# Two buffers of P in the last two pairs, the third for raw weights, and later turns for weight preparation

## The chip, the cores and the metric

One core of one Trainium2 chip runs the whole program in one launch. The metric is device microseconds of one execution. Matrix products run on TensorE (PE), elementwise work on VectorE (DVE), ScalarE (ACT) and GpSimd (POOL); every DMA is issued by SyncE (SP), one queue in program order. A time counts as changed if it moves by more than 0.5%, about 3.8 us here.

## The reference, cut to what matters

```python
# attention, 2 batches x 8 heads, 768 tokens, head size 64
q_bits = (q @ proj) > 0            # 6 bits: a bucket for each query and each key
mask   = q_bucket[:, None] == k_bucket[None, :]
P      = softmax(where(mask, q @ k.T / 8, -1e9))
x      = P @ v                     # as 1536 tokens x 512
# two feed-forward layers, 512 -> 2048 -> 512
y   = leaky(x @ moe_w_in, 0.01)  @ moe_w_out
out = prelu(y @ moe2_w_in, alpha) @ moe2_w_out
```

The program is handed the four weight matrices in float64, the rest in float32; it reads the two 32-bit words of a weight with integer operations.

## The kernel before

**Attention.** Heads go in 8 pairs (NP = 8), a pair being two heads of one batch; a pair has 12 score tiles, numbered `g = 12 * i + m`, so there are N = 96 of them. A tile (`score`) is 128 queries by 768 keys of one head: scores on PE, a capped minimum on DVE (L717), the exponential on ACT (L720). Then its P is turned over, keys onto partitions: either by three PE transposes and an ACT copy out of PSUM, twice (L736, L741), or by a split into a float16 high and low part (L754, L758, L760) and a DMA transpose (L766). A pair has two halves of 384 queries (f = 0, 1). The turned-over P of a half fills one tile of the ring `pt`, three buffers of 4608 words a partition, taken in turn (L703). `pv` multiplies it by v (L807, L816) and DVE writes x (L823); after that the buffer is free. Below, pv(6,1) is the product for pair 6, half 1.

**Feed-forward.** `ffn` walks 16 units (layer l, quarter fq of the 2048 hidden columns, batch b). A unit multiplies x by the quarter's w_in (`product`, L1163 to L1166, output named h, or y where it lies in the second bank of a y tile), applies the leaky step, and the next unit's steps take turns with the unit's own products with w_out (`y_group`). Where fq is 0 a unit uses the four blocks of x as they are (B11, B21, B12, B22); where it isn't, seven products that also need sums of blocks (T1 to T4, `x_sum`, L1150). Each block is split into two float16 parts (`x_keep`, `halves`: ACT L1087, DVE L1089).

**Group preparation.** The weights come in 16 groups, one for each layer, quarter and matrix: group 0 is the first quarter of the first w_in, group 1 that of the first w_out. `convert(n, claim, step, early)` loads four raw 512 KB tiles (L987), makes float32 of each (ACT L993; DVE L995, L999, L1002, L1005), finds one power of two for the group (`power`: DVE L933 to L944, a diagonal on ACT or POOL, a PE product L950, DVE L954 to L959), and splits the weights with it (L1087, L1089). Groups 0 and 1 convert one raw tile at a time, the others two.

**Memory is lent on.** When the attention has no more use for a buffer, the feed-forward takes it: raw tiles of groups 0 and 1 take three slots of `wraw`, then four of pt buffer 2, then the first of `wraw` again. So three tiles of group 0 lie in `wraw`, its fourth and three of group 1 in pt buffer 2. Split w_out lies in pt buffer 1, and some of the activations in pt buffer 0. Sixteen halves through three buffers: the last user of buffer 2 is pv(7,0), of buffer 1 pv(6,1), of buffer 0 pv(7,1).

**Who sets the order.** Every step is an operation added to a plan with a claim, possible engines with a modelled duration, what it reads and writes, and a turn (the claim unless given). `link` walks operations by claim: this fixes who waits for whom on a buffer. `first` builds a schedule from the modelled durations; among ready operations of one engine that could start within a short span, the lowest turn goes first. `late` and `early` then move each operation as late as its users allow and as early as its engine allows, by turns; of all schedules the one with the earliest modelled end is kept (`order`), and each engine's instructions are issued in its order. The chip follows that order whatever the real durations are.

Claims of the feed-forward start at N + 10 = 106. Before the change group 0 has claim 104 (its first three tiles 36), group 1 claim 105; conversion takes those claims as turns:

```python
convert(0, at - 2, 0.2, N - 60)
convert(1, at - 1, 0.2)
```

Of the kernel before, what the change touches and what calls it, by code (L numbers as in the profile page):

```python
# [43 lines left out]
LEAN_V, LEAN_X, LEAN_W = 0.0,0.0,0.0  # L44

X_LEAD, CONV = 30, (2, 5, 19, 6)
START, XAT = 10.0, (1, 9)
# [258 lines left out]
def lsh_attention_ffn_kernel(  # L306
# [13 lines left out]
    nc = tc.nc  # L320
# [51 lines left out]
    hl_r = ring("hl", 2)  # L372
    pt_r = ring("pt", 3)

    def fixed(shape, dtype, name, p=const):
# [318 lines left out]
    def score(g):  # L694
# [6 lines left out]
        if (i, f) not in sums:  # L701
            sums[i, f] = sum_r.new([128, TH, 2], F32, "sum")
            pts[i, f] = pt_r.new([128, 4 * T, HALF], F16, "pt")  # L703
        sm, pt = sums[i, f], pts[i, f]
# [172 lines left out]
    class Bank:  # L877
# [8 lines left out]
        def ap(self, w=HALF):  # L886
# [14 lines left out]
    thin_slots = Slots(list(zip(small[0::2], small[1::2])))  # L901
    w_outs = views(pt_at[1], 2 * T * HALF, DM)[:2 * FQ]
    o_slots = Slots(list(zip(w_outs[0::2], w_outs[1::2])))
# [3 lines left out]
    gv = [v for b in s_at[1:] for v in views(b, S, HALF // 2)]  # L907
    gv += views(pt_at[0], 2 * T * HALF, HALF // 2)[:16]
    g_slots = Slots(list(zip(gv[0::2], gv[1::2])))
    h_slots = Slots([v for b in (s_at[0], *v_at) for v in views(b, S, HALF)]  # L910
                    + [View(pt_at[0], 8 * HALF + n * HALF, HALF) for n in range(4)])
    m_slots = Slots(views(on(m_r, 0, DM), DM, DM))
    m_pairs = Slots(views(on(hl_r, 1, 2 * S), 2 * DM, 2 * DM))

    def bank(ring):
        return Bank(ring.new([128, 1, HALF], F32, "h"), 0)
# [7 lines left out]
    def power(claim, cols_, most, most_use, scale_, scale_use, extra=None, reads=(), writes=(), wide=False, to=2.0**13):  # L924
# [3 lines left out]
        mx = mx_r.new([128, 1], F32, "mx")  # L928
        ps = b_banks.take() if claim >= N + 2 else bank(t_ps)
        buf, n = cols_  # L930
# [31 lines left out]

        plan.add(claim, vec(0.95 if extra else 0.8, scales), [ps.use(), *reads], [most_use, scale_use, *writes])

    def convert(n, claim, step, early=None):

# [4 lines left out]
        for k in range(FQ // per):  # L971
            j = k * per
            first = claim + j * step if early is None or j == FQ - 1 else early
            now = claim + j * step
            r, m = (r_slots.take(), m_slots.take()) if per == 1 else (r_pairs.take(), m_pairs.take())
            each = [View(r.buf, r.c0 + a * 2 * DM, 2 * DM) for a in range(per)]
            for a, one in enumerate(each):
# [16 lines left out]
                out=m.ap(F32), in_=high().bitcast(F32), func=AF.Abs)), [r.use()], [m.use()], turn=now)  # L994
            plan.add(first, vec(0.24 + w * 0.00052, lambda m=m, k=k: nc.vector.tensor_scalar(  # L995
                out=m.ap(F32), in0=m.ap(F32), scalar1=F64_MAX, scalar2=F64_MIN, op0=ALU.min,
                op1=ALU.max, accum_out=mw.t[:, k:k + 1]), True),
                [m.use()], [m.use(), col(mw, k)], turn=now)
            plan.add(first, vec(0.18 + w * 0.00052, lambda m=m: nc.vector.tensor_scalar(  # L999
                out=m.ap(I32), in0=m.ap(I32), scalar1=3, scalar2=0x3FFFFFFF,  # L1000
                op0=ALU.logical_shift_left, op1=ALU.bitwise_and), True), [m.use()], [m.use()], turn=now)
            plan.add(first, vec(0.19 + w * 0.00104, lambda m=m, low=low: nc.vector.scalar_tensor_tensor(  # L1002
                out=low(), in0=low(), scalar=29, in1=m.ap(I32), op0=ALU.logical_shift_right,
                op1=ALU.bitwise_or), True), [m.use(), r.use()], [r.use()], turn=now)
            plan.add(first, vec(0.19 + w * 0.00104, lambda low=low, high=high: nc.vector.scalar_tensor_tensor(  # L1005
                out=low(), in0=high(), scalar=-0x40000000, in1=low(), op0=ALU.bitwise_and,
# [39 lines left out]
        for p in range(0, FQ, 2):  # L1046
# [16 lines left out]
            for out_, x, y, op, to, frm in (  # L1063
                (s1, a21, a22, ALU.add, r1, r2), (s3, a11, a21, ALU.subtract, r2, r1),
                (s2, s1, a11, ALU.subtract, r1, r1), (s4, a12, s2, ALU.subtract, r2, r1),
            ):
                def add(out_=out_, x=x, y=y, op=op, eng=None):
                    eng.tensor_tensor(out=out_(), in0=x(), in1=y(), op=op)
                plan.add(claim, [
                    vec(0.37, lambda add=add: add(eng=nc.vector), True),  # L1070
                    gps(0.7, lambda add=add: add(eng=nc.gpsimd))], [r1.use(), r2.use()], [to.use()])
            halves(claim, wide, lambda r1=r1: r1.ap(F32).rearrange("p (d two) -> p two d", two=2),
# [72 lines left out]
    def x_sum(b, nm, claim, turn):  # L1145
# [3 lines left out]
        op = ALU.add if nm == "T2" else ALU.subtract  # L1149
        plan.add(claim, [vec(0.95, lambda: nc.vector.tensor_tensor(out=o(), in0=x(), in1=y(), op=op), True),  # L1150
                         gps(1.9, lambda: nc.gpsimd.tensor_tensor(out=o(), in0=x(), in1=y(), op=op))],
# [31 lines left out]
    def leaky(u, f, n, claim, src, src_use, own=None):  # L1183
# [7 lines left out]
        else:  # L1191
            plan.add(claim, act(0.58, lambda: nc.scalar.activation(
                out=g.ap(F32), in_=src(), func=AF.Copy, scale=low_by.t[:, f:f + 1])),
                [src_use, low_by], [g.use()])
            plan.add(claim, vec(0.56, lambda: nc.vector.scalar_tensor_tensor(  # L1195
                out=g.ap(F32), in0=src(), scalar=high_by.t[:, f:f + 1], in1=g.ap(F32),
# [130 lines left out]
    def ffn():  # L1327
# [5 lines left out]
        for u in [(l, fq, b) for l in range(2) for fq in range(NFQ) for b in range(B)]:  # L1333
            l, fq, b = u
            m = l * NFQ + fq
            if b == 0 and m == 0:
                convert(0, at - 2, 0.2, N - 60)
                convert(1, at - 1, 0.2)
            if b == 0 and m + 1 < 2 * NFQ:
# [80 lines left out]
```

## Time and profile before

| | us |
|---|---|
| three runs: median (lowest to highest) | 761.66 (761.4 to 764.04) |
| the profiled execution | 758.8 |
| its span, first to last instruction | 757.0 |
| PE busy (idle) | 705.5 (51.5) |
| DVE, ACT, POOL busy | 624.1, 487.7, 312.9 |

Attention fills the span up to about 252 us, the feed-forward the rest. PE is busy for 93% of the span and nowhere fully idle for long, so the time can only change by what stands between its instructions, or by its clock.

### The profile page before, as it was taken

What the parts mean: (1) busy time and instruction counts of PE and PEld (TensorE: products, weight loads), DVE (VectorE), ACT (ScalarE), POOL (GpSimd) and SP (SyncE); (2) the same over time, 40 slices, a digit from 0 to 9 for tenths busy, and PEclk for the clock granted to TensorE, in tenths of its full rate; (3) what the DMA queues carried; (4) which work ended last, traced back from release to release, by engine and by line L of the source; (5) the groups of instructions that cost most, each with busy time, mean ns of one, the idle gap of its engine ahead of it and who ended that gap; (6) DMA issues with size and microseconds to landing.
All of it is one profiled execution on the core that took longest, in us unless ns stands there. A gap on an engine that the chain in (4) does not pass through costs nothing.

```text
span 757.0 us, 12700 instructions
## 1 busy us (share of the span) xinstructions
PE 705.5 (93%) x4727; PEld 448.2 (59%) x4727; DVE 624.1 (82%) x1105; ACT 487.7 (64%) x903; POOL 312.9 (41%) x316
## 2 busy tenths in 40 slices
PE   7789978988987799999999999999999999999997
PEld 5577767877876556655565556555454555555553
DVE  6889898788899987879888886999997989986442
ACT  5887878897889676666656545565675764654340
POOL 2776757866564052213332532324043324333220
PEclk9989999999999899999999999999999999999999
DMA  7597997988757430331322313120311212100012
GB/s 208 126 197 166 194 197 168 221 173 177 157 129 145 171 103 9 111 113 41 106 77 74 95 56 111 34 78 1 112 52 60 84 59 82 55 1 2 15 55 98
DMA packets 131214, 77.89 MB, mean 103 GB/s; under 512 B 100864, under 2 KB 123392, under 8 KB 131152
## 3 DMA queue, kind: packets, MB, share of 16 engines
q1 hardware_dynamic: 131152, 77.08, 39.3%
q8 instruction: 37, 0.61, 0.3%
q14 instruction: 25, 0.20, 0.1%
HBM read 43.00 MB, written 3.15 MB: 61 GB/s over the span
## 4 chain that ended last, share of the span: by engine, by line
PE 66%; DVE 25%; ACT 4%; issue 3%; POOL 1%; DMA 0%; SPq 0%; DVEq 0%; POOLq 0%
PE y L1164 10%; PE y L1166 10%; PE y L1165 10%; PE sc L710 7%; PE h L1164 6%; PE h L1166 6%; PE h L1165 6%; DVE ff L1089 4%; PE o L807 3%; DVE s L717 3%; PE pp L736 2%; PE o L816 2%; DVE ff L995 2%; DVE ff L1002 2%; DVE hl L760 2%
## 5 line engine op out<-in xcount | busy, mean ns | idle before, releaser
L416 POOL TENSOR_TENSOR ff<-ff 128x384 f16<-128x384 f32 x128 | 138.4, 1095 | 282.2 <-ACT ff L1198 241.9
L1164 PE MATMUL y<-ff 128*128 128x384 f16 (+1 forms) x496 | 171.9, 347 | 9.4 <-DVE ff L1209 2.8
L1166 PE MATMUL y<-ff 128*128 128x384 f16 (+1 forms) x496 | 171.8, 346 | 0.0
L1165 PE MATMUL y<-ff 128*128 128x384 f16 (+1 forms) x496 | 171.8, 346 | 0.0
L1164 PE MATMUL h<-ff 128*128 128x384 f16 x416 | 136.3, 328 | 2.9 <-ACT ff L1087 2.8
L1165 PEld LDWEIGHTS <-ff 128*128 128x128 f16 x912 | 89.4, 98 | 81.1 <-issue 14.9
L1166 PE MATMUL h<-ff 128*128 128x384 f16 x416 | 136.2, 327 | 0.7 <-DVE ff L1089 0.7
L1165 PE MATMUL h<-ff 128*128 128x384 f16 x416 | 136.1, 327 | 0.0
L1164 PEld LDWEIGHTS <-ff 128*128 128x128 f16 x912 | 89.3, 98 | 71.3 <-ACT ff L1087 2.9
L1166 PEld LDWEIGHTS <-ff 128*128 128x128 f16 x912 | 89.3, 98 | 70.6 <-DVE ff L1089 1.1
L717 DVE TENSOR_SCALAR_CACHE_REDUCE s<-sc 128x768 f32<-128x768 f32 x96 | 89.6, 951 | 19.1 <-PE sc L710 13.1
L720 ACT ACTIVATE s<-s,mn 128x768 f32<-128x768 f32 x96 | 89.6, 935 | 13.2 <-DVE s L717 12.5
L1298 DVE SCALAR_TENSOR_TENSOR x<-y,back,x 128x384 f32<-128x384 f32 (+1 forms) x84 | 56.3, 670 | 37.9 <-PE y L1166 35.1
L1198 ACT CAST ff<-ff 128x384 f16<-128x384 f32 x128 | 64.6, 510 | 23.2 <-DVE ff L1195 21.2
L1205 ACT COPY ff<-h 128x384 f32<-128x384 f32 x72 | 34.1, 477 | 56.1 <-PE h L1166 55.0
L710 PE MATMUL sc<-ka,qa 128*128 128x384 f32 x192 | 59.8, 394 | 8.8 <-DVE s L717 8.6
L416 POOL TENSOR_TENSOR hl<-s,hl 128x768 f16<-128x768 f32 x31 | 53.1, 1712 | 30.0 <-ACT hl L754 29.9
L710 PE MATMUL sc<-kb,qb 76*128 76x384 f32 x192 | 51.7, 350 | 0.2 <-ACT kb L613 0.2
L1089 DVE SCALAR_TENSOR_TENSOR ff<-ff,by 128x512 f16<-128x512 f32 (+2 forms) x54 | 48.1, 919 | 3.3 <-ACT ff L1087 3.1
L1087 ACT ACTIVATE ff<-ff,by 128x512 f16<-128x512 f32 (+2 forms) x54 | 43.7, 863 | 10.0 <-DVE by L959 8.2
L807 PE MATMUL o<-pt,vb 128*64 128x256 f16 (+1 forms) x576 | 48.2, 276 | 0.0
L1002 DVE SCALAR_TENSOR_TENSOR ff<-ff 128x1024 int32<-128x1024 int32 (+1 forms) x36 | 45.9, 1275 | 0.8
(142 smaller groups left out, 1207.2 us busy)
## 6 DMA issues: line engine op xcount, KB each, us to landing
ff<-in_moe_w_in_dram SPq DMA_DIRECT2D x32, 512.0 KB
ff<-in_moe_w_out_dram SPq DMA_DIRECT2D x32, 512.0 KB
v<-in_v_dram SPq DMA_DIRECT2D x8, 384.0 KB
out_dram<-x SPq DMA_DIRECT2D x12, 256.0 KB
k<-in_k_dram SPq DMA_DIRECT2D x7, 384.0 KB
q<-in_q_dram SPq DMA_DIRECT2D x7, 384.0 KB
kb<-ka SPq DMA_DIRECT2D x14, 192.0 KB
qb<-qa SPq DMA_DIRECT2D x14, 192.0 KB
```

The lines of the kernel that those rows point to most:

```text
L416: nc.gpsimd.tensor_tensor(out=o, in0=a, in1=b, op=ALU.subtract)
L710: nc.tensor.matmul(sc.t[:, h, 0:HALF], lhsT=o[a].t[0:rows, row:row + 128], rhs=o[b].t[0:rows, h * HALF:h * HALF + HALF], start=(n == 0), s ...
L717: plan.add(g, vec(1.03, lambda: nc.vector.tensor_scalar(out=s.t.rearrange("p (a b) -> p a b", a=2), in0=sc.t[:, :, 0:HALF], scalar1=FILL, ...
L720: plan.add(g, act(1.12, lambda: nc.scalar.activation(out=s.t, in_=s.t, func=AF.Exp, scale=-1.0, bias=mn.t[:, 0:1], accum_out=sm.t[:, t, j: ...
L807: nc.tensor.matmul(ps.t[64 * j:64 * j + 64, 0:split], lhsT=vb.t[:, piece, j, c, :], rhs=narrow(pt, i, f)[:, 2 * T * j + o + c], start=(c + ...
L1002: plan.add(first, vec(0.19 + w * 0.00104, lambda m=m, low=low: nc.vector.scalar_tensor_tensor(out=low(), in0=low(), scalar=29, in1=m.ap(I3 ...
L1089: plan.add(claim, vec(0.2 + w * 0.00108, lambda: nc.vector.scalar_tensor_tensor(out=part(lo), in0=src(), scalar=c(), in1=part(hi), op0=ALU ...
L1164: nc.tensor.matmul(ps, lhsT=lh[0], rhs=rh[0], start=first, stop=False, skip_group_check=skip)
L1165: nc.tensor.matmul(ps, lhsT=lh[0], rhs=rh[1], start=False, stop=False, skip_group_check=skip)
L1166: nc.tensor.matmul(ps, lhsT=lh[1], rhs=rh[0], start=False, stop=last, skip_group_check=skip)
L1198: plan.add(claim, act(0.51, lambda: nc.scalar.copy(out=gh.ap(), in_=g.ap(F32))), [g.use()], [gh.use()])
L1298: plan.add(claim, vec(0.69 if l else 0.56, lambda: nc.vector.scalar_tensor_tensor(out=a(), in0=ps.ap(w), scalar=c(), in1=a(), op0=ALU.mult ...
```

## The change

It has five parts.

1. From pair 6 on, the turned-over P takes buffers 0 and 1 in turn; buffer 2 is used last by pv(5,1). The split w_out moves from buffer 1 to 0, the activations from 0 to 1. Buffer 0's last user is now pv(7,0), buffer 1's pv(7,1).
2. `EARLY`: group 0 has claim 88 and its fourth raw tile claim 78; group 1 keeps claim 105 but its raw tiles have claims 80, 80, 80, 90. The turn of the conversions of both is 104 (of their loads 98); what follows in `convert`, the power of two and the split, has the claim as its turn: 88.6 to 88.8 for group 0.
3. `LAG`: in groups 2 to 15 every operation but the loads has its turn 6 later.
4. Modelled durations of nine kinds of operation are changed.
5. The PE product of `power` no longer takes the two second banks of the y tiles in turn with the units' own use: group scales always take the first, the others the second. Group 0's takes a bank of the ring ps_t, as its claim lies before N + 2.

```diff
+LAG = 6
+EARLY = (88, 0.2, (36, 36, 36, 78)), (105, 0.2, (80, 80, 80, 90))
...
+    pt_late = part(pt_r, 0, 1)
...
-            pts[i, f] = pt_r.new([128, 4 * T, HALF], F16, "pt")
+            pts[i, f] = (pt_r if i < NP - 2 else pt_late).new([128, 4 * T, HALF], F16, "pt")
...
-    w_outs = views(pt_at[1], 2 * T * HALF, DM)[:2 * FQ]
+    w_outs = views(pt_at[0], 2 * T * HALF, DM)[:2 * FQ]
...
-    gv += views(pt_at[0], 2 * T * HALF, HALF // 2)[:16]
+    gv += views(pt_at[1], 2 * T * HALF, HALF // 2)[:16]
...
-                    + [View(pt_at[0], 8 * HALF + n * HALF, HALF) for n in range(4)])
+                    + [View(pt_at[1], 8 * HALF + n * HALF, HALF) for n in range(4)])
...
-        ps = b_banks.take() if claim >= N + 2 else bank(t_ps)
+        ps = b_banks.got[0 if wide else 1] if claim >= N + 2 else bank(t_ps)
...
-    def convert(n, claim, step, early=None):
+    def convert(n, *args):
+        first = len(plan.ops)
+        convert_now(n, *args)
+        for op in plan.ops[first:]:
+            if n > 1 and op.ways[0][0] != "SP":
+                op.turn += LAG
+
+    def convert_now(n, claim, step, early=None):
...
-            first = claim + j * step if early is None or j == FQ - 1 else early
-            now = claim + j * step
+            first = claim + j * step if early is None else early[j]
+            now = N + 8 if per == 1 else claim + j * step
...
-                convert(0, at - 2, 0.2, N - 60)
-                convert(1, at - 1, 0.2)
+                convert(0, *EARLY[0])
+                convert(1, *EARLY[1])
```

The changed durations, in us, w being the columns (512 or 1024): L995 from 0.24 + 0.00052 w to 0.2 + 0.00105 w, L999 from 0.18 + 0.00052 w to 0.13 + 0.00071 w, L1002 and L1005 from 0.19 + 0.00104 w to 0.13 + 0.00123 w and 0.13 + 0.0012 w; the scales of `power` (L963) from 0.8 or 0.95 to 1.0 or 1.2; weight sums (L1070) from 0.37 to 0.47 on DVE and from 0.7 to 0.8 on POOL; x sums (L1150) from 0.95 to 1.1; the leaky step of layer 1 (L1195) from 0.56 to 0.6 or 0.68.

## Rows read from the trace of the kernel before

**Rows 1.** Windows: start:end, length, busy PE, PEld, DVE, ACT, POOL, PEclk, DMA, GB/s
```profile
220.00:260.00 40.00, 30.31 (x309) 23.89 (x304) 38.37 (x78) 31.71 (x59) 12.78 (x12) 0.93 0.49 124
260.00:280.00 20.00, 18.83 (x114) 11.11 (x112) 18.59 (x40) 13.74 (x27) 8.16 (x8) 0.98 0.28 90
280.00:300.00 20.00, 20.00 (x125) 12.03 (x123) 16.48 (x17) 12.95 (x22) 9.07 (x7) 1.00 0.23 84
...
257.04:735.90 478.86, 465.91 (x2674) 261.93 (x2675) 398.94 (x660) 282.36 (x488) 156.10 (x152) 1.00 0.20 66
```

**Rows 2.** PE timeline, 205 to 285 us: start, us, line, count, [idle before, releaser]
```profile
220.31 0.39 PE L816 MATMUL o<-pt,v 128*64 128x128 f32 x4
...
232.80 0.39 PE L816 MATMUL o<-pt,v 128*64 128x128 f32 x4
...
244.22 0.55 PE L736 MATMUL pp<-ident,s 128*128 128x128 f32 x3 [0.63 <-ACT pt L741]
246.25 0.55 PE L736 MATMUL pp<-ident,s 128*128 128x128 f32 x3 [1.48 <-ACT pt L741]
...
253.93 0.33 PE L950 MATMUL y<-dg,ones 128*128 128x128 f32 x1 [1.25 <-ACT dg L621]
257.04 0.34 PE L1164 MATMUL h<-ff 128*128 128x384 f16 x1 [2.78 <-ACT ff L1087]
...
258.23 0.50 PE L1166 MATMUL h<-ff 128*128 128x384 f16 x1 [0.70 <-DVE ff L1089]
...
261.15 0.33 PE L1164 MATMUL h<-ff 128*128 128x384 f16 x1
...
261.64 0.33 PE L1164 MATMUL h<-ff 128*128 128x384 f16 x1
```

**Rows 3.** Chain of waits, 232 to 262 us: start, us, what ended last
```profile
247.69 2.78 DVE ff L1089 x3
250.47 0.61 DVE ff L995 x2
```

**Rows 4.** ACT timeline, 150 to 290 us
```profile
224.53 0.48 ACT L741 COPY pt<-pp 128x384 f32<-128x384 f32 x1 [1.27 <-PE pp L736]
...
233.69 0.48 ACT L741 COPY pt<-pp 128x384 f32<-128x384 f32 x1
...
244.06 1.77 ACT L1087 ACTIVATE ff<-x,x_by 128x768 f16<-128x768 f32 x2
...
248.56 0.66 ACT L993 ACTIVATE ff<-ff 128x512 f32<-128x512 f32 x1
```

**Rows 5.** SP timeline, 200 to 285 us (x5 merges issues and the waits between)
```profile
213.17 28.25 SPq L766 DMA_TRANSPOSE pt<-hl  x5
243.16 0.39 SPq L410 DMA_DIRECT2D ff<-in_moe_w_in_dram  x1
```

**Rows 6.** DMA view, 240 to 262 us: GB/s in 40 slices of 0.55 us
```profile
GB/s 290 290 289 280 120 0 0 39 136 303 363 439 402 425 417 417 425 387 60 0 0 0 0 0 0 0 0 0 0 0 0 0 0 0 67 216 387 358 290 343
```

**Rows 7.** Groups of instructions by form: busy us, mean ns, idle before
```profile
L1002 DVE SCALAR_TENSOR_TENSOR ff<-ff 128x1024 int32<-128x1024 int32 x28 | 38.9, 1390 | 0.7
...
L1005 DVE SCALAR_TENSOR_TENSOR ff<-ff 128x1024 int32<-128x1024 int32 x28 | 38.0, 1356 | 0.4
...
L995 DVE TENSOR_SCALAR_CACHE_REDUCE ff<-ff 128x1024 f32<-128x1024 f32 x28 | 33.9, 1209 | 3.2 <-ACT ff L993 3.2
...
L999 DVE TENSOR_SCALAR ff<-ff 128x1024 int32<-128x1024 int32 x28 | 23.9, 853 | 0.5
```

**Rows 8.** Waits of PE, 275 to 720 us: total us, times, longest
```profile
PE y L1164 <- DVE ff L1209: 2.8, 4, 1.0
PE y L1164 <- DVE biggest L954: 2.4, 5, 0.8
```

**Rows 9.** Timelines around the start of unit (0,1,0): DVE, 300 to 310; PE, 310 to 320
```profile
309.05 1.28 DVE L1089 SCALAR_TENSOR_TENSOR ff<-ff,by 128x1024 f16<-128x1024 f32 x1 [0.70 <-ACT ff L1087]
...
312.47 0.33 PE L1164 MATMUL h<-ff 128*128 128x384 f16 x1
```

More of the change, by code (lines that the diff above doesn't have):

```diff
@@ L961, in scales @@
                 extra()
-        plan.add(claim, vec(0.95 if extra else 0.8, scales), [ps.use(), *reads], [most_use, scale_use, *writes])
-    def convert(n, claim, step, early=None):
+        plan.add(claim, vec(1.2 if extra else 1.0, scales), [ps.use(), *reads], [most_use, scale_use, *writes])
+    def convert(n, *args):
[5 more added lines that the diff above has]
+    def convert_now(n, claim, step, early=None):
         l, fq, nm = groups[n]
@@ L994, in convert @@
                 out=m.ap(F32), in_=high().bitcast(F32), func=AF.Abs)), [r.use()], [m.use()], turn=now)
-            plan.add(first, vec(0.24 + w * 0.00052, lambda m=m, k=k: nc.vector.tensor_scalar(
+            plan.add(first, vec(0.2 + w * 0.00105, lambda m=m, k=k: nc.vector.tensor_scalar(
                 out=m.ap(F32), in0=m.ap(F32), scalar1=F64_MAX, scalar2=F64_MIN, op0=ALU.min,
@@ L998, in convert @@
                 [m.use()], [m.use(), col(mw, k)], turn=now)
-            plan.add(first, vec(0.18 + w * 0.00052, lambda m=m: nc.vector.tensor_scalar(
+            plan.add(first, vec(0.13 + w * 0.00071, lambda m=m: nc.vector.tensor_scalar(
                 out=m.ap(I32), in0=m.ap(I32), scalar1=3, scalar2=0x3FFFFFFF,
                 op0=ALU.logical_shift_left, op1=ALU.bitwise_and), True), [m.use()], [m.use()], turn=now)
-            plan.add(first, vec(0.19 + w * 0.00104, lambda m=m, low=low: nc.vector.scalar_tensor_tensor(
+            plan.add(first, vec(0.13 + w * 0.00123, lambda m=m, low=low: nc.vector.scalar_tensor_tensor(
                 out=low(), in0=low(), scalar=29, in1=m.ap(I32), op0=ALU.logical_shift_right,
                 op1=ALU.bitwise_or), True), [m.use(), r.use()], [r.use()], turn=now)
-            plan.add(first, vec(0.19 + w * 0.00104, lambda low=low, high=high: nc.vector.scalar_tensor_tensor(
+            plan.add(first, vec(0.13 + w * 0.0012, lambda low=low, high=high: nc.vector.scalar_tensor_tensor(
                 out=low(), in0=high(), scalar=-0x40000000, in1=low(), op0=ALU.bitwise_and,
@@ L1069, in convert @@
                 plan.add(claim, [
-                    vec(0.37, lambda add=add: add(eng=nc.vector), True),
-                    gps(0.7, lambda add=add: add(eng=nc.gpsimd))], [r1.use(), r2.use()], [to.use()])
+                    vec(0.47, lambda add=add: add(eng=nc.vector), True),
+                    gps(0.8, lambda add=add: add(eng=nc.gpsimd))], [r1.use(), r2.use()], [to.use()])
             halves(claim, wide, lambda r1=r1: r1.ap(F32).rearrange("p (d two) -> p two d", two=2),
@@ L1149, in x_sum @@
         op = ALU.add if nm == "T2" else ALU.subtract
-        plan.add(claim, [vec(0.95, lambda: nc.vector.tensor_tensor(out=o(), in0=x(), in1=y(), op=op), True),
+        plan.add(claim, [vec(1.1, lambda: nc.vector.tensor_tensor(out=o(), in0=x(), in1=y(), op=op), True),
                          gps(1.9, lambda: nc.gpsimd.tensor_tensor(out=o(), in0=x(), in1=y(), op=op))],
@@ L1194, in leaky @@
                 [src_use, low_by], [g.use()])
-            plan.add(claim, vec(0.56, lambda: nc.vector.scalar_tensor_tensor(
+            plan.add(claim, vec(0.6 if own is None else 0.68, lambda: nc.vector.scalar_tensor_tensor(
                 out=g.ap(F32), in0=src(), scalar=high_by.t[:, f:f + 1], in1=g.ap(F32),
```

## The prediction

> **What bounds the kernel now.** I read the windows first. Over the feed-forward, 257.0 to 735.9 us, PE is busy for 465.9 of 478.9 us [rows 1]: this stage is bound by PE, and whatever lets it start earlier is kept to the end as long as its inputs keep up. The loose place is where attention passes into it: from 220 to 260 us PE is busy for 30.3 of 40 us, DVE for 38.4, and the granted clock is 0.93, while from 280 to 300 PE has no idle time [rows 1]. So next the PE timeline there. Attention's PE work, pv(7,1) last, ends at 252.7 (253.93 less the 1.25 us of idle before it) [rows 2]. Then PE waits 1.25 us for the diagonal of group 0's scale, 2.78 us for the first split weight and 0.70 us for its low part [rows 2]. The chain of waits says what is late: DVE splits x, then at 250.47 converts a raw tile [rows 3]. ACT began that tile at 248.56 [rows 4], and its load was issued at 243.16, behind the last transpose [rows 5]. It is the fourth raw tile of group 0, which lies in pt buffer 2 and so had to wait for pv(7,0). Everything else of the first unit was there.
>
> **The change part by part.** Durations are of the profiled execution, 758.8 us (span 757.0). It is 2.9 us below the median of the runs, 761.66; I carry the difference in us over to the median.
>
> *Group 0's fourth tile and group 1's tiles earlier.* Buffer 2 is now free after pv(5,1), three halves sooner than pv(7,0), so the load can be issued among the transposes of pairs 6 and 7 and the tile converted before attention ends. The number of instructions stays the same. What goes is idle time: 1.25 + 2.78 + 0.70 = 4.7 us [rows 2]. After it PE also ran slowly: from 257.04 to 261.15 it did four triples of products, the wait of 0.70 us among them; the next starts 0.49 us after it, at 261.64 [rows 2], so 4.11 - 0.70 - 4 x 0.49 = 1.45 us were lost: a product lasts 0.50 us at 258.23 and 0.33 at 261.15 [rows 2]. That is the lower of the clock's two levels, 1.2 against 2.4 GHz, after 4 us with almost nothing to do; windows with less idle show a granted clock of 1.00 [rows 1]. With PE going from pv(7,1) straight into the unit, both go: **-6.2 us**. Bounds: nothing, if DVE is late in another way (first rival), and -6.2.
>
> *The end of attention itself.* PE idles for 0.63 and 1.48 us behind ACT's copies of P [rows 2]; ACT was splitting x in between, 1.77 us from 244.06 [rows 4], work that was free to go there only because the plan held the load to be late. The window's 0.93 [rows 1] says that a part of pv(7,1) behind these gaps is at the lower clock too. Now group 0's own split competes for ACT, so I don't take the two idles for gone. Bounds 0 and -3.6 (2.1 of idle, and an estimate of 1.5 of clock, the loss found above); I take **-1**.
>
> *Two buffers of P.* The new wait stands before the first writes of P of a half: DMA transposes on SP's queue (what is behind it there: later transposes, and the loads) and copies on ACT (behind it: exponentials). Pair 7's first half now waits for pv(6,0), whose last row starts at 220.31 and lasts 0.39 us; its first copy is at 224.53 [rows 2, 4]: 3.8 us of cover. The second half waits for pv(6,1), last row at 232.80 for 0.39 us; first copy at 233.69: 0.5 us of cover. Bounds 0 (the order stays) and +2 (one step of P waits for a whole product later); I take **+0.5**, near the rows. Split w_out now waits for pv(7,0), long before group 1 is split; activations have pv(7,1) as before.
>
> *Four loads among the transposes.* Between 243 and 250 us the four loads move 2.1 MB in 12 slices of 0.55 us, most at 400 GB/s or more [rows 6]: 1.3 to 1.65 us each. The SP queue holds five transposes and the waits between them for 28 us [rows 5], and the DMA engines are busy for 0.49 of 220 to 260 us [rows 1], so there is room. Bounds 0 and 6.6 us, all four ahead of one late transpose; I take **+0.5**.
>
> *What DVE must do first.* DVE has 1.6 us of idle time in 220 to 260 and 1.4 in 260 to 280 [rows 1], so conversions can only come forward if something steps back. Something can: about eight sums and splits of x for T1 to T4 of batch 0, some 0.93 us each (2.78 / 3) [rows 3], run in this stretch and are first used at 312.47, in unit (0,1,0) [rows 9]: 7.4 us, as much as the 6.2 that are to be won. Then DVE has 3.5 us of idle time in 280 to 300 [rows 1]. It fits with little to spare: bounds 0 and +6.2, I take **+1**.
>
> *New durations and LAG.* For a pair of raw tiles the plan counted 0.77 + 0.71 + 1.255 + 1.255 = 3.99 us; the rows say 1.209 + 0.853 + 1.390 + 1.356 = 4.81 [rows 7], and the new formulas 4.87. With 28 pairs DVE fell 23 us behind the plan over the feed-forward, and PE, kept in the planned order, waited for sums and scales: the largest are 2.8 and 2.4 us [rows 8], of 13 us of idle time in all [rows 1]. Truer durations and a later turn for the conversions should take some of it. Bounds -5 (the two rows gone) and +7.2 (third rival); I take **-2**. The fixed banks of `power` change only which product waits behind a scale; its waits are the 2.4 us over five times, bounds -2.4 and +2.4, and I take 0.
>
> Sum: -6.2 - 1 + 0.5 + 0.5 + 1 - 2 = -7.2. The profiled execution would take 751.6, the median **754.5 us**.
>
> **The rivals.**
>
> *DVE becomes the bound (same).* If DVE does all that it did before unit (0,1,0) and loses only the little idle time, group 2's first split still ends at 309.05 + 1.28 = 310.3 and the unit starts 2.1 us earlier than 312.47 [rows 9], whatever was won at 257: 761.7 - 2.1 = 759.5. For it: DVE at 38.4 of 40 and 18.6 of 20 [rows 1]. Against: the sums that can step back.
>
> *Loads hold up the transposes (same).* All of these go through one queue, and four loads ahead of pair 7's last transpose delay it by up to 6.6 us [rows 6], which pv(7,1) and the first unit inherit: -7.2 + 6.6, or 761. Against it stands the DMA share of 0.49. The Trainium skill, "DMA: Bandwidth & Descriptors", section "Queues, rings and completion order", states that each DMA engine takes the descriptors of a queue in order; by that rule, a load ahead is paid in full by the transpose behind it. The trace agrees so far that the tile issued at 243.16 behind a transpose was begun only 5.4 us later.
>
> *Weights come too late (slower).* LAG puts a group's conversions six claims back. The feed-forward has 306 claims (24 + 3 x 44 + 30 + 3 x 40, from the steps of `ffn`) in 478.9 us, 1.56 us each, so 9.4 us. If the finish of group 2 moved by that, from 310.3 to 319.7, unit (0,1,0) would start 7.2 us later than now; what was won before it is lost as well: 761.7 + 7.2 = 769. It decides from a slip of 2.1 us. For it: that small margin. Against: the turn only chooses among operations that are ready, the later passes go by slack, and DVE has idle time from 280 on.
>
> *More is won (faster).* Attention's end gives its 3.6 and the feed-forward 5: -6.2 - 3.6 - 5 = -14.8, or 747. For it: truer durations act on all groups. Against: DVE is nearly full wherever two groups meet.
>
> **How the numbers follow.** A change within 0.5%, 3.8 us, can't be told from none. Forecast 0.50 (its own range 751 to 758), more won 0.13, DVE bound 0.15, loads 0.07, late weights 0.15. Faster: nearly all of the forecast and of the fourth rival, 0.62. Slower: most of the late weights and a little of the planner's other ways to reorder, 0.14. The same: 0.24. The range goes from 747 to 765: the lower end of the fourth rival and the worst of the third are left out.
>
> **What would show it.** Right: the fourth tile of group 0 is loaded before 240 us, no idle of over 1 us stands between pv(7,1) and the first h product, that product comes by 252 us at the full clock, and unit (0,1,0) starts near 306. Two buffers wrong: ACT or SP waits for pv(6,1). DVE bound: first h early, but a wait of several us for a split weight at unit (0,1,0). Late weights: such waits at later units too. I would be wrong if attention ended later than 252.7 by more than was won, or if the feed-forward's own waits grew beyond 13 us.

## The result, and the profile after

| | before | after |
|---|---|---|
| median of 9 runs each on the same chip, us | 761.4 (758.92 to 764.04) | 766.83 (764.7 to 772.19) |
| ratio | 1 | 1.0083, interval [1.0057, 1.0108] |
| profiled execution (span), us | 758.8 (757.0) | 766.36 (764.3) |
| PE, DVE, ACT, POOL busy, us | 705.5, 624.1, 487.7, 312.9 | 709.7, 625.7, 490.2, 302.2 |

It is 0.8% slower where 0.9% faster was forecast. After's lines are 3 higher in attention (L710 is L713) and 10 higher in the feed-forward (L1164 is L1174). To see where the time went, I count the feed-forward's 912 triples (a triple is the three matmuls of L1164 to L1166) on PE and note when some of them start:

| start of triple, us | 1st | 49th | 701st | 912th | 49th to 701st | 701st to 912th |
|---|---|---|---|---|---|---|
| before | 257.04 | 284.12 | 631.12 | 752.37 | 347.00 | 121.25 |
| after | 258.38 | 291.87 | 634.29 | 759.77 | 342.42 | 125.48 |

After is 7.75 us behind at the 49th triple, wins 4.58 in the middle and gives back 4.23 in the last quarter. So there are two losses and one gain. Each row is one execution: two pairs of kernels below that share PE's order up to the 49th triple (k7 and before; k4 and k19, but for three instructions) start it 1.9 and 2.6 us apart, so a difference of that size is not sure. The windows of after, columns as in [rows 1], show the first loss; the last line is the window of before that [rows 1] does not have:

```profile
180.00:220.00 40.00, 28.26 (x256) 22.46 (x256) 33.81 (x67) 31.96 (x63) 18.43 (x20) 0.90 0.92 198
220.00:260.00 40.00, 31.74 (x223) 24.67 (x221) 31.97 (x68) 29.38 (x57) 14.26 (x14) 0.80 0.51 124
260.00:280.00 20.00, 19.42 (x222) 14.29 (x219) 17.52 (x38) 13.22 (x25) 4.76 (x6) 1.00 0.11 31
```

```profile
180.00:220.00 40.00, 36.17 (x321) 30.66 (x323) 33.97 (x62) 32.40 (x65) 24.44 (x25) 0.91 0.82 176
```

From 180 to 220 PE is busy for 28.3 us (before 36.2), and from 220 to 260 DVE for 32.0, against 38.4 in [rows 1]: neither engine is full, something holds up both. PE's largest waits of after (us in total, times, longest) and its rows there:

```profile
PE sc L713 <- DVE s L720: 9.4, 14, 1.7
PE o L810 <- DMA pt<-hl: 8.4, 1, 8.4
...
PE y L1174 <- DVE ff L1219: 3.4, 5, 0.7
```

```profile
219.82 0.85 PE L810 MATMUL o<-pt,vb 128*64 128x256 f16 x6 [8.44 <-DMA pt<-hl]
...
258.38 0.32 PE L1174 MATMUL h<-ff 128*128 128x384 f16 x1 [0.81 <-ACT rs L800]
```

One wait of 8.44 us for a transpose; behind it six matmuls that take 0.52 us in k1 below take 0.85, and the granted clock of 220 to 222 us is 0.50, the lower level (1.2 GHz). SP's queue says why, where [rows 5] had transposes only:

```profile
203.61 0.40 SPq L413 DMA_DIRECT2D ff<-in_moe_w_in_dram  x1
204.06 0.50 SPq L413 DMA_DIRECT2D ff<-in_moe_w_out_dram  x1
...
205.17 1.37 SPq L413 DMA_DIRECT2D ff<-in_moe_w_out_dram  x2
206.65 8.46 SPq L769 DMA_TRANSPOSE pt<-hl  x1
...
219.22 27.35 SPq L769 DMA_TRANSPOSE pt<-hl  x3
```

All four early loads, with one move of q among them, stand right ahead of one transpose of pair 6. In the chain of waits this transpose takes 13.12 us from its issue:

```profile
206.65 13.12 DMA pt<-hl
219.82 0.85 PE o L810 x6
```

And three of the four were not urgent. ACT's first conversions of early tiles in after (L1003 is L993 of [rows 4]):

```profile
222.51 0.67 ACT L1003 ACTIVATE ff<-ff 128x512 f32<-128x512 f32 x1
...
261.43 0.67 ACT L1003 ACTIVATE ff<-ff 128x512 f32<-128x512 f32 x1
264.21 0.69 ACT L1003 ACTIVATE ff<-ff 128x512 f32<-128x512 f32 x1
```

Group 0's fourth tile is converted soon after the wait, the first w_out tile some 57 us after its load. (`Line.early` lets a later DMA slip into a gap of the modelled transfers ahead of an earlier one; in this trace it stood behind it.)

The second loss, in the last quarter, is short waits; after's PE:

```profile
664.73 0.32 PE L1174 MATMUL y<-ff 128*128 128x384 f16 x1 [0.84 <-DVE x L1308]
667.32 0.38 PE L1174 MATMUL y<-ff 128*128 128x512 f16 x1 [0.65 <-DVE ff L1219]
700.32 0.38 PE L1174 MATMUL y<-ff 128*128 128x512 f16 x1 [0.65 <-DVE ff L1219]
718.39 0.38 PE L1174 MATMUL y<-ff 128*128 128x512 f16 x1 [0.72 <-DVE ff L1219]
733.86 0.38 PE L1174 MATMUL y<-ff 128*128 128x512 f16 x1 [0.72 <-DVE ff L1219]
```

They sum to 3.58 us; of such waits over 0.2 us before has one of 0.31 in its last quarter.

### The profile page after: what moved, and what is told of

Same layout as the page of the kernel before. It is cut to its first block, busy times and chain, and to the rows that moved or that the text cites. A ratio compares the mean times of both kernels' runs of the same rounds, so it can differ in the third digit from the quotient of the medians.

```text
span 764.3 us, 12699 instructions
## 1 busy us (share of the span) xinstructions
PE 709.7 (93%) x4727; PEld 450.7 (59%) x4727; DVE 625.7 (82%) x1109; ACT 490.2 (64%) x912; POOL 302.2 (40%) x303
## 4 chain that ended last, share of the span: by engine, by line
PE 69%; DVE 19%; ACT 4%; issue 3%; DMA 3%; POOL 2%; SPq 0%; DVEq 0%; POOLq 0%; ACTq 0%
PE y L1174 10%; PE y L1176 10%; PE y L1175 10%; PE h L1174 8%; PE h L1175 7%; PE h L1176 7%; PE sc L713 5%; PE o L810 4%; DVE s L720 3%; DVE ff L1099 3%; DMA pt<-hl 3%; PE o L819 2%; PE tp L542 2%; PE pp L739 2%; DVE ff L1012 2%
## 5 line engine op out<-in xcount | busy, mean ns | idle before, releaser
L419 POOL TENSOR_TENSOR ff<-ff 128x384 f16<-128x384 f32 x128 | 134.4, 1062 | 297.3 <-ACT ff L1208 224.0
L1174 PE MATMUL y<-ff 128*128 128x384 f16 (+1 forms) x496 | 171.9, 347 | 8.8 <-DVE ff L1219 3.4
L1174 PE MATMUL h<-ff 128*128 128x384 f16 x416 | 135.7, 326 | 2.8 <-DVE ff L1205 1.1
L1174 PEld LDWEIGHTS <-ff 128*128 128x128 f16 x912 | 89.2, 98 | 68.3 <-issue 0.3
L713 PE MATMUL sc<-ka,qa 128*128 128x384 f32 x192 | 60.4, 397 | 9.5 <-DVE s L720 9.4
L810 PE MATMUL o<-pt,vb 128*64 128x256 f16 (+1 forms) x576 | 50.4, 286 | 8.4 <-DMA pt<-hl 8.4
L1099 DVE SCALAR_TENSOR_TENSOR ff<-ff,by 128x512 f16<-128x512 f32 (+2 forms) x54 | 52.3, 997 | 4.3 <-ACT ff L1097 4.3
L713 PE MATMUL sc<-kb,qb 76*128 76x384 f32 x192 | 52.4, 354 | 0.3 <-ACT kb L616 0.3
L1012 DVE SCALAR_TENSOR_TENSOR ff<-ff 128x1024 int32<-128x1024 int32 (+1 forms) x36 | 50.1, 1392 | 0.9
```

The costliest lines, as they stand in the source:

```text
L419: nc.gpsimd.tensor_tensor(out=o, in0=a, in1=b, op=ALU.subtract)
L713: nc.tensor.matmul(sc.t[:, h, 0:HALF], lhsT=o[a].t[0:rows, row:row + 128], rhs=o[b].t[0:rows, h * HALF:h * HALF + HALF], start=(n == 0), s ...
L810: nc.tensor.matmul(ps.t[64 * j:64 * j + 64, 0:split], lhsT=vb.t[:, piece, j, c, :], rhs=narrow(pt, i, f)[:, 2 * T * j + o + c], start=(c + ...
L1012: plan.add(first, vec(0.13 + w * 0.00123, lambda m=m, low=low: nc.vector.scalar_tensor_tensor(out=low(), in0=low(), scalar=29, in1=m.ap(I3 ...
L1099: plan.add(claim, vec(0.2 + w * 0.00108, lambda: nc.vector.scalar_tensor_tensor(out=part(lo), in0=src(), scalar=c(), in1=part(hi), op0=ALU ...
L1174: nc.tensor.matmul(ps, lhsT=lh[0], rhs=rh[0], start=first, stop=False, skip_group_check=skip)
```

## The experiments

Each kernel was run beside the kernel before, whose median was 759.46 to 759.78 us; ratios are to it, with their intervals.

### Are the four loads what costs?

**k1** moves, in the finished order of the changed kernel, only the three w_out loads (group 1's tiles 0 to 2) behind the first transpose of pair 7:

```
+MOVED = [(("raw", 1, 0), ("turn", 7, 0, 0)), (("raw", 1, 1), ("raw", 1, 0)), (("raw", 1, 2), ("raw", 1, 1))]
```

> The changed kernel in the very order that it has, but for three DMA issues: the loads of the first three w_out tiles of group 1 stand behind the first transpose of pair 7 instead of ahead of the first transpose of pair 6's second query tile. Theory 1 (the queue): the transpose issued at 206.65 us landed 13.1 us later because four loads of 512 KB stood ahead of it in the one queue, and PE idled 8.4 us for it and then ran some 12 us at the half clock. Then that wait falls below 2 us and the time to 755 to 759 us, against 766.8 for the changed kernel. Theory 2 (two buffers of P, or the order in which attention and feed-forward are interleaved, cost the time): PE waits there as long for something else, and the time stays above 763.

Measured: 762.09 us, ratio 1.0021 [1.0, 1.0041]: between the two ranges. The instructions of PE, DVE, ACT and POOL stand in the order of after, and the 912th triple starts 4.71 us earlier. On PE, and once on ACT, in k1:

```profile
212.29 0.52 PE L818 MATMUL o<-pt,vb 128*64 128x256 f16 x6 [0.53 <-DMA pt<-hl]
215.91 0.90 PE L746 MATMUL pp<-ident,s 128*128 128x128 f32 x3 [2.88 <-ACT pt L751]
...
231.48 0.62 PE L720 MATMUL sc<-ka,qa 128*128 128x384 f32 x2 [1.99 <-DVE s L727]
...
233.78 0.47 PE L961 MATMUL h<-dg,ones 128*128 128x128 f32 x1 [1.26 <-ACT dg L631]
```

```profile
212.92 2.58 ACT L1106 ACTIVATE ff<-x,x_by 128x768 f16<-128x768 f32 x3
```

8.44 us became 0.53; part of it came back as other waits. The one of 2.88 us is for a copy of P on ACT, and right ahead of that copy ACT does 2.58 us of splits of x.

**k2** puts all four loads directly behind the transpose that was late.

```
+MOVED = [(("raw", 0, 3), ("turn", 6, 0, 1)), (("raw", 1, 0), ("raw", 0, 3)), ...]
```

> The changed kernel in its order, but all four early loads stand directly behind the late transpose instead of ahead of it, so ahead of the four small moves of the bucket bits for pair 7. If transfers go in the order of issue (theory 1), the transpose lands about 5 us after its issue, the 8.4 us wait of PE is gone, the bucket bits come some 6 us later instead and pair 7's first scores may wait 0 to 5 us: 757 to 763 us. If the transfers merely share the DMA engines, whichever is issued first (theory 3), the transpose still takes 10 us or more, PE waits over 4 us for it, and the time is 764 or more.

Measured: 764.81, ratio 1.0071 [1.0047, 1.0094]. The time lies in the range given for shared engines (764 or more), but the wait of over 4 us that this theory needs is absent. PE in k2:

```profile
210.93 0.52 PE L818 MATMUL o<-pt,vb 128*64 128x256 f16 x6
...
215.14 0.90 PE L746 MATMUL pp<-ident,s 128*128 128x128 f32 x3 [3.47 <-ACT pt L751]
...
219.71 0.98 PE L720 MATMUL sc<-kb,qb 76*128 76x384 f32 x2 [0.99 <-DMA ff<-in_moe_w_out_dram]
```

The wait for the transpose is gone, so it was the place in the queue; but the loads now stand ahead of what comes next: scores wait 0.99 us with a load named as releaser, and P's PE transposes 3.47 us for ACT.

### Which part of the change does what?

**k3** is before plus parts 3 to 5 (LAG, durations, banks), **k4** before plus parts 1 and 2 (two buffers, early turns). Of the lines of the change they hold:

```
# k3
+LAG = 6
+vec(0.2 + w * 0.00105, ...
+ps = b_banks.got[0 if wide else 1] if claim >= N + 2 else bank(t_ps)
# k4
+EARLY = (88, 0.2, (36, 36, 36, 78)), (105, 0.2, (80, 80, 80, 90))
+pts[i, f] = (pt_r if i < NP - 2 else pt_late).new(...)
```

> The kernel before with parts 3, 4 and 5 of the change (LAG, modelled durations, banks of the power of two), without the two buffers of P and without EARLY. If these parts won in the feed-forward what the changed kernel made up there (it was 7.8 us behind after the transition and 3.2 us behind at three quarters): 757 to 759 us. If they are worth nothing: 760 to 763. If late weights were a cause of the loss: above 764.

Measured: 769.62, ratio 1.0135 [1.0096, 1.0174]: in the range of late weights, but not for that reason.

> The kernel before with parts 1 and 2 of the change (two buffers of P in the last two pairs, early loads), old durations, no LAG, old banks. Its plan has one early load ahead of a transpose of pair 6 and three ahead of the bucket bits of pair 7. Theory 1 (the queue): these moves come 4 to 8 us late and PE idles for them, 762 to 770 us. As the prediction had it (the loads hide among the transposes): 753 to 757.

Measured: 760.12, ratio 1.002 [0.999, 1.005]: in neither range. k3's loss is in attention: scores wait 15.3 us for DVE (8.6 in before), and the 49th triple starts at 297.43. k4's starts at 279.70, 4.4 us ahead of before, though PE waits 3.98 us for a transpose behind one load; then 3.9 of it goes in the last quarter (347.00 us from the 49th to the 701st triple, as before, and 125.17 from there).

**k6** is before plus the durations, **k7** before plus LAG, **k9** the changed kernel with the old durations:

```
# k6 (and, turned round, k9), in all places of the change
-vec(0.24 + w * 0.00052, ...
+vec(0.2 + w * 0.00105, ...
# k7
+                op.turn += LAG
```

> The kernel before with only the new durations (part 4); loads, buffers, turns and banks are those of before. Theory that the durations are what reordered attention in k3: 767 to 771 us, ratio 1.010 to 1.015, with waits of 10 us and more in sum of scores on DVE before 205 us. Rival (the later turn did it): 757 to 761, ratio 0.997 to 1.002, attention in the order of before. My forecast's term, -2 from durations and turn together, would give 757 to 760.

Measured: 765.07, ratio 1.0085 [1.0058, 1.0112]: between the ranges.

> The kernel before with only the later turn of the conversions of groups 2 and up (LAG of 6). Theory that the durations reordered attention: this one is 758 to 762 us, ratio 0.998 to 1.003, with attention's milestones within 1.5 us of before. Rival (the turn did it): 766 to 771, ratio 1.008 to 1.015. Late weights (my third rival): attention as before, and waits of several us of PE for split weights from the third group on, +3 to +7 us at the end.

Measured: 759.28, ratio 1.0004 [0.9978, 1.003], as expected.

> The changed kernel with the old durations alone; two buffers, early turns, LAG and banks kept. Theory that the durations cost what k3 lost, and that they cost as much in the changed kernel: 759 to 762 us, near k4. Rival (the changed kernel's loss is the four loads alone, and the durations only decide where these are put): it goes by where the loads stand here; with a wait of 4 us or more of o for a transpose 762 to 767, with none 754 to 758.

Measured: 761.39, ratio 1.0031 [1.0007, 1.0056], in the first range; there is a wait of 5.3 us, but of P's PE transposes for ACT, not of o for a transpose. So LAG does nothing that can be measured, and the new durations alone lose 0.85%, 6.5 us (5.3 between the medians). They act far from the conversions: the order of k6's instructions differs from that of before from the first heads on, PE's order in k7 only from the first products of group 2. Of the 6.1 us by which k6's 912th triple is late, 4.3 are lost in the last quarter, in five waits (three of 0.65 us for the line of DVE that the next section is about, two of 0.84 for its writes of x).

**k14** asks whether that is the durations or just another order: before, with the planner's choice restricted.

```
-PATIENCE, PASSES = (0.05, 0.1, 0.15, 0.2, 0.25, 0.3), 7
+PATIENCE, PASSES = (0.05,), 7
```

> The kernel before, whose planner is allowed the patience 0.05 alone, so that another of its own candidate orders is emitted; loads, buffers, turns, durations and banks are those of before. Theory that the new durations cost 6.5 us in k6 by letting another candidate win, and that candidates lie as far apart on the chip as that: this one is 764 to 770 us, ratio 1.005 to 1.014. Rival (the durations themselves do harm, candidates with the old ones lie close together): 758 to 762, ratio 0.998 to 1.003.

Measured: 763.3, ratio 1.0048 [1.0027, 1.0069]: between the two ranges, 0.7 us below the one and 1.3 above the other. Another order of the same kernel, with the same durations, costs 3.7 us (before its first triple PE waits 4.89 us for a diagonal and 2.47 for the first split). More than half of k6's loss is thus no more than a change of order can cost by itself; what the durations do beyond that stays open.

### The last quarter: a PSUM bank

k4's last quarter is 3.92 us longer than before's. PE's waits for one line of DVE, in k4 and in two kernels below, k11 and k19 (us in total, times, longest):

```profile
PE y L1166 <- DVE ff L1211: 7.1, 10, 0.7
```

```profile
PE y L1164 <- DVE ff L1209: 7.9, 11, 0.8
```

```profile
PE y L1166 <- DVE ff L1211: 2.7, 4, 0.9
```

L1209, where it reads y, sums the third of the seven products (`p2`) out of PSUM. `p2` writes one half of a PSUM tile from `b_banks`, each y group the other half of one from `y_banks`; there are two such tiles, taken in turn. In before `power` takes a step of `b_banks` too. k4's claim 88 for group 0 is below N + 2, so there that step is not taken, and for the rest of the kernel every `p2` sits in the other tile. **k11** is before with that step alone:

```
+        b_banks.take()          # at the start of ffn
```

> The kernel before with one line: the ring of PSUM banks that the third product of h and power share is turned by one extra step at the start of the feed-forward, so that this product and the y groups around it trade places in the two PSUM tiles. Nothing else changes. Bank theory (a y group that takes the tile in which DVE still sums the product before it waits for that sum): the waits of y on DVE ff L1209 grow from 2.8 us in 4 to some 7 us in 10, as in k4, and the time by 4 to 5 us: 763.5 to 766, ratio 1.004 to 1.008. Rival (these waits come from the order in which the sums were planned, not from the bank): 759 to 761, ratio 0.998 to 1.002, waits as before. My forecast for the banks was 0 with bounds of 2.4 us either way.

Measured: 766.1, ratio 1.0085 [1.0054, 1.0117], a little more than expected. The instructions of PE, DVE, ACT and POOL stand in the order of before. PE and DVE of k11, then PE and DVE of before at the same place; the first PE line of each is the end of `p2`'s product:

```profile
715.96 0.33 PE L1166 MATMUL y<-ff 128*128 128x384 f16 x1
716.12 0.38 PE L1164 MATMUL y<-ff 128*128 128x512 f16 x1
716.34 0.38 PE L1165 MATMUL y<-ff 128*128 128x512 f16 x1
716.55 0.38 PE L1166 MATMUL y<-ff 128*128 128x512 f16 x1
717.65 0.38 PE L1164 MATMUL y<-ff 128*128 128x512 f16 x1 [0.72 <-DVE ff L1209]
```

```profile
717.04 0.56 DVE L1209 TENSOR_TENSOR ff<-y,ff 128x384 f32<-128x384 f32 x1 [2.89 <-PE y L1166]
```

```profile
711.05 0.33 PE L1166 MATMUL y<-ff 128*128 128x384 f16 x1
...
711.64 0.38 PE L1166 MATMUL y<-ff 128*128 128x512 f16 x1
711.86 0.38 PE L1164 MATMUL y<-ff 128*128 128x512 f16 x1
```

```profile
711.48 0.56 DVE L1209 TENSOR_TENSOR ff<-y,ff 128x384 f32<-128x384 f32 x1 [2.24 <-PE y L1166]
```

In k11 the second triple of the y group starts 0.05 us after DVE's sum ends (717.04 + 0.56); in before it follows the first at once. The sum itself is held up as well. In before it starts 0.10 us after `p2`'s product (711.05 + 0.33), beside the y group; in k11 that product ends at 716.29 and DVE is idle, but the sum starts only at 717.04, 0.11 us after the y group's first triple (716.55 + 0.38). So PE and DVE take turns at a tile although each uses its own half: in ten of k11's eleven waits, and in all five of after's, the sum starts 0.04 to 0.11 us after a triple of y. Why the program waits for a whole tile the trace doesn't show; the planner counts the halves as separate (`Bank.use`), so its order does not allow for it. The Trainium skill, "Perfetto Trace Analysis", section "Matmuls", asks that independent matmul groups rotate through PSUM banks so that their evacuation overlaps the next group; both kernels rotate, and k11 shows that the phase of the two rotations counts as well.

**k12** chooses the tile by the next y group, in k4:

```
-                ps = b_banks.take()
+                ps = b_banks.got[(y_banks.i + 1) % 2]
```

> k4 (two buffers and early turns alone) with one line changed: the third product of h takes the PSUM tile that the next y group does not use. Bank theory: the waits of y on DVE ff (7.1 us in 10) fall to 2 to 3 us, and the gain that k4 had at the 48th triple reaches the end: 754.5 to 757, ratio 0.993 to 0.998. Rival (DVE is full, and what is won at the transition is handed back to it whatever the banks): the waits change their line and the time stays at 759 to 761.

Measured: 759.85, ratio 1.0004 [0.9979, 1.0029], the rival's range. The waits fell to 2.3 us, but the planner, which sees the other tile, emitted another order with a new wait of 5.54 us in attention. **k15** and **k18** are the same line in the changed kernel and in before.

> The changed kernel with one line changed: the third product of h takes the PSUM tile that the next y group does not use. Attention is emitted in the same order. Bank theory: the last 211 triples of the feed-forward, 125.5 us in the changed kernel against 121.2 before, take 121 to 122; time 761.5 to 763.5, ratio to before 1.002 to 1.006. Rival (the last quarter is slower for its conversions that come later, by LAG): no change, 765.5 to 767.5, ratio 1.007 to 1.010.

Measured: 771.8, ratio 1.0168 [1.0131, 1.0206], the wrong way: the last quarter took 122.98 us, as the bank theory has it, but the order is another one from the start of the feed-forward, with four such waits from 344 to 406 us. A line that changes the plan isn't a test of the bank.

> The kernel before with the third product of h in the PSUM tile that the next y group does not use. It had few such waits, 2.8 us in 4; bank theory: 757 to 759.5, ratio 0.996 to 1.000. If it is faster than that, the banks alone are worth more than the waits that the profile names. Rival: within 0.2% of before.

Measured: 757.98, ratio 0.9986 [0.996, 1.0011]: within both ranges, and its order is another one too.

**k16** is k15 with k1's late loads.

> k15 with the three loads of w_out behind the first transpose of pair 7, as in k1. If the loads and the banks are the two terms that my forecast had wrong and they add up (4.7 and 4 us): 757 to 759.5, ratio 0.996 to 1.000, the kernel before or slightly faster. Rival (they share one cover, DVE): as the better of k1 and k15, 761 to 763, ratio 1.001 to 1.004.

Measured: 765.54, ratio 1.0078 [1.0049, 1.0108]: neither expectation, since k15 was slower itself. But the loads are worth 6.3 us there (771.8 to 765.54), which agrees with k1.

### Can the early turns win?

**k5** is k4 with the three w_out loads behind the first transpose of pair 7 (k1's line); **k13** is k12 with the four loads behind two transposes of pair 6; **k17** is k13 with one ACT copy moved ahead of four splits of x:

```
# k13
+MOVED = [(("raw", 0, 3), ("turn", 6, 0, 1)), (("raw", 1, 0), ("turn", 6, 1, 0)), ...]
# k17
+        op = ops.pop(1072)
+        ops.insert(1046, op)
```

> Buffers and early turns with the durations, the turn and the banks of before; the order is that of k4, but the three loads of w_out stand behind the first transpose of pair 7, and only the load of w_in is left ahead of the transposes. Queue theory (a load ahead of a transpose is paid in full, the early turns gain for themselves): the wait of 3.98 us at o L809 falls below 1.5 us, and 2.5 to 4 us of it reach the end: 756 to 757.5, ratio to before 0.994 to 0.998. Rival (DVE is full, so what is won at the transition is handed back in the feed-forward, as in k4): the wait goes and the time stays at 759 to 760.5, ratio 0.999 to 1.002.

Measured: 761.72, ratio 1.0027 [1.0002, 1.0052]. Neither theory: the wait stayed (3.93 us), as the w_in load alone causes it, and the moved loads held up a later transpose for 2.42 us.

> k12 with its four early loads placed so that no transpose that is waited for stands behind them: the load of group 0's fourth tile behind the last transpose of pair 6's first half, the three of w_out behind the first transpose of pair 6's second half, where SP waits anyway. Queue theory: the wait of 3.98 us of o for a transpose falls below 1 us, and 2.5 to 4 us of it reach the end: 751 to 754, ratio 0.989 to 0.994, faster than the kernel before. Rival (as in k5, the loads only hold up a later transpose or a move of q and k): a wait of 2 us and more appears elsewhere, and the time is that of k12 within 1 us.

Measured: 760.06, ratio 1.0003 [0.9977, 1.003], k12's time, as the rival said. No wait for a transpose is left, but k12 had none either; its wait for ACT stays; ACT and PE of k13:

```profile
209.20 3.40 ACT L1098 ACTIVATE ff<-x,x_by 128x768 f16<-128x768 f32 x4
212.50 0.46 ACT L750 COPY pt<-pp 128x384 f32<-128x384 f32 x1
```

```profile
213.01 0.90 PE L745 MATMUL pp<-ident,s 128*128 128x128 f32 x3 [5.54 <-ACT pt L750]
```

> k13 (two buffers, early turns, better banks, loads behind transposes that nothing waits for) with one copy of P on ACT moved ahead of four splits of x. Theory (ACT's splits of x, put there because the plan holds the next transpose to be late, hold up PE): the wait of 5.54 us of pp L745 falls below 2 us, and 3 to 5 us reach the end: 755 to 757, ratio 0.993 to 0.997, faster than both kernels. Rival (PE only waits for the next thing in line, DVE or the transpose): the wait changes its name, and the time stays within 1.5 us of k13, 758.5 to 761.5.

Measured: 760.03, ratio 1.0007 [0.9981, 1.0033], the rival. In k17 the next copy waits behind the same splits:

```profile
209.95 0.52 PE L820 MATMUL o<-pt,vb 128*64 128x256 f16 x6 [1.05 <-DMA pt<-hl]
214.22 0.90 PE L748 MATMUL pp<-ident,s 128*128 128x128 f32 x3 [3.53 <-ACT pt L753]
```

**k19** therefore leaves the plan alone: k4 with k11's line, which puts every `p2` back into the tile of before. PE's order is k4's but for three instructions, ACT's and DVE's are k4's. **k20** also places the loads as k13.

> k4 (two buffers and early turns alone) with the one line of k11: an extra step of the ring of PSUM banks at the start of the feed-forward. The order of instructions is that of k4 but for 3 of PE. Bank theory: k4's 10 waits of y on DVE ff (7.1 us) fall to about 4 (2.8 us), and since nothing is planned anew, 4 us reach the end: 755 to 757, ratio 0.994 to 0.997. Rival (what is won is handed back in any order): 759 to 761.

Measured: 753.85, ratio 0.9928 [0.9899, 0.9958], a little faster than expected; before 759.7.

> k19 with its four early loads behind transposes that nothing waits for (one behind the last transpose of pair 6's first half, three behind the first of pair 6's second half). Queue theory: k4's wait of 3.98 us of o for a transpose falls below 1.5 us, and another 2 to 4 us reach the end: 751.5 to 754.5, ratio 0.989 to 0.993, faster than both kernels. Rival (PE then waits for DVE, ACT or the moves of q and k instead): within 1 us of k19.

Measured: 754.76, ratio 0.9908 [0.9879, 0.9938]. Both beat both kernels, before and after. k20 can't be told from k19: its wait for the transpose halved to 2.01 us, and PE got a wait of 2.07 for ACT in return, as the rival said.

```profile
211.08 0.52 PE L817 MATMUL o<-pt,vb 128*64 128x256 f16 x6 [2.01 <-DMA pt<-hl]
214.43 0.90 PE L745 MATMUL pp<-ident,s 128*128 128x128 f32 x3 [2.07 <-ACT pt L750]
```

## Why the prediction was wrong

**"Four loads among the transposes", +0.5, is the failed step that an experiment isolates.** It measured +4.7 us (k1), 6.3 in k16's order: within the bounds of 0 and 6.6, so it was taking a value near 0 that failed. I read a DMA share of 0.49 as room, but that is the share of 220 to 260 us; the loads were issued from 203.6 to 206 us, and from 180 to 220 us the share was 0.82 in before already. And room in the engines says nothing of the place in a queue. The rival had the mechanism; I gave it 0.07. PE's wait was 8.44 us, and PE then ran at the lower clock, with a granted 0.50. The Trainium skill, "DMA: Bandwidth & Descriptors", section "Queues, rings and completion order", cited there, has the engine take a queue's descriptors in order; the runs agree (13.12 us from issue to use behind four loads, some 5.4 in k1, where o could start at 212.29 after an issue at 206.86).

**"The fixed banks ... I take 0"** failed in its reason. I held them to change only which product waits behind a scale. They set the tile in which `p2` sits against the y groups: k11, that and nothing else, costs 6.5 us; in the changed kernel four such waits stand in the last quarter, 2.74 us of its 4.23, and k9, with the same banks and the old durations, has 14 of them, 8.7 us. The row was in front of me [rows 8]: I took 2.8 us of waits for L1209 as DVE running late. In before that is so for three of the four sums, which DVE began without idle time; what I missed is that the placement decides whether PE waits for a sum at all (k11). How much the changed kernel would win with other banks in one and the same order was not measured.

**"New durations and LAG", -2.** In the feed-forward the direction seems right: in the changed kernel the 49th to the 701st triple take 4.58 us less than before, while with the old durations (k9) that stretch takes 349.26 us, more than before's 347.00. But I let part 4 act in the feed-forward alone. It changes the planner's order everywhere, and alone it costs 6.5 us (k6). LAG costs nothing (k7); the rival of late weights did not occur.

**The transition is the largest miss of the sum: "Group 0's fourth tile and group 1's tiles earlier", -6.2, with -1 for the end of attention, +0.5 for the two buffers and +1 for DVE, -5.7 together.** In k1, without the large wait, the 49th triple is 3.0 us later than before (287.12 against 284.12), 8.7 us from the forecast. What failed is "PE going from pv(7,1) straight into the unit". Attention's last product ends at 252.21 us in before, but at 271.87 in after and at 267.12 in k1, with seven triples of the feed-forward run ahead of it. Waits of 2.88, 1.99 and 1.26 us for ACT and DVE stand inside pairs 6 and 7 instead of the 4.7 at the start of the feed-forward: idle time of PE from 180 us to the 49th triple, summed from windows of 2 us, is 14.9 us in k1 and 14.7 in before. So in the changed kernel the forecast's idle time moved ahead rather than went. The other 2.8 us are busy time, at a granted clock of 0.89 against 0.92 from 180 to 260 us. Why the stretch got longer stays open: 3.0 us is little more than two executions of one order differ by, and with the old durations kernels with the same early turns start the 49th triple earlier than before does (k4 by 4.4 us, k9 by 1.6), so the order that the new durations gave to attention may have its part. DVE being the bound (759.5) is not shown: DVE had more idle time than before.

**What held.** The fourth tile was loaded before 240 us and no wait of over 1 us stood before the first h product; but this came at 258.38, not 252, and the 107th triple, with which unit (0,1,0) starts in before, at 320.22, not 306. k19, parts 1 and 2 with `p2` in the tile of before, is 0.72% faster, 5.5 us, and the five terms of these parts add up to -6.2 - 1 + 0.5 + 0.5 + 1 = -5.2. That is in part luck: a wait of 3.98 us behind a load is still in k19, where I took 0.5, its order is not that of before, and the trace places the gain elsewhere: from DVE's 60th score tile to the 49th triple k19 wins 2.7 us and up to the 701st another 2.3. The two buffers of P made neither ACT nor SP wait for pv(6,1) in a row that I found. Two slips moved nothing: six of the twelve slices reach 400 GB/s, not most [rows 6], and the new formulas give 4.88, not 4.87.

The whole difference at the 912th triple, +7.40 us in these two traces (5.4 between the medians), is thus: the loads +4.75; what is left of the transition +3.00; the feed-forward -0.35, a gain of 4.58 in its middle and a loss of 4.23 at its end. The first is shown by k1 and k2. The second stays open. That the middle's gain comes of the durations is supported by k9 alone, and the plan is another one there too. That the loss at the end comes of the banks is argued, from k11 and k19, from k9 (125.64 us for that stretch with the old durations) and from k7 (121.18 with LAG alone); no run changed the banks of the changed kernel and kept its order.

## What to carry to other kernels

Before a load is moved ahead, look at what is issued behind it on the same queue and who waits for that: the load belongs behind it, however idle the DMA engines are, and not ahead of the next thing that is waited for (k2, k5). Where a planner orders the work, test an edit in the finished order as well, or the time of another order is measured with it. When a short wait of one length keeps coming back on one line, compare where both sides lie in PSUM before calling the engine late.

## What the runs showed of the hardware that I had not expected

After the wait of 8.44 us the granted clock was 0.51 from 219.8 to 226 us and 1.00 from 226 to 232: some 6 us at the lower level, not the 12 that I gave with k1. The mean of 220 to 260 us fell from 0.93 [rows 1] to 0.80, but only in part by that wait: k1, without it, has 0.85. k4 and k19 share PE's order there but for three instructions, and yet the granted clock from 180 to 260 us was 0.96 in the one and 0.91 in the other.

Issuing a transpose took SP 3.0 to 4.1 us for 28 of the 31 in before (the longest 6.18) and 3.41 in k1 with a load and a move of q ahead; right behind one load it took 5.26 (k4), behind two 7.15 (k9) and behind four 8.46.

PE and DVE took turns at a PSUM tile of which each used its own half: DVE's sum began 0.11 us after PE's triple, PE's next triple 0.05 us after the sum (k11).
